# Clearing a dead strip on Pool between the row scatters of chunks 1 to 3 of an attention and mixture-of-experts kernel

## The chip, the cores and the metric

The kernel runs on one core of one Trainium2 chip. The metric is the device time in microseconds (us) of one execution; lower is better. Every run is also recorded with its span and with the clock that TensorE was granted, as a share of full speed. A run counts as slow when it is over 1.5% above the fastest of the same kernel. The numbered runs (e1 to e18) were made on four different chips of the same kind, here called 0, 3, 9 and 10; for the two profiles and the comparison of record the chip isn't noted. Kernels of one call share a chip and the runs of the kernel before on it.

## The reference

Attention over keys and values that a softened sorting matrix has mixed, then a one-expert-per-row feed-forward layer. Cut to what matters:

```python
# q, k, v: (4, 8, 768, 64); sort_net: (4, 8, 8, 8)
k_sorted = einsum('bhij,bhjcd->bhicd', P, k_b)      # P: five rounds of softmax on sort_net
v_sorted = einsum('bhij,bhjcd->bhicd', P, v_b)
attn = softmax(q_b @ k_sorted.T / 8)                # inside blocks of 96 rows
x = (attn @ v_sorted) as 3072 rows of 512
# feed-forward: 8 experts, 512 -> 1024 -> 512
e_idx = argmax(x @ w_gate + modality_bias[modality_id])
for e in range(8):
    rows = e_idx == e
    out[rows] = gate[rows] * (relu(x[rows] @ w1[e]) @ w2[e])
```

## The kernel before

The 3072 rows are handled as four chunks, m = 0 to 3. When a chunk's attention is done, `place(m)` computes for each row its place in a list sorted by expert, and Pool writes the rows there with eight indirect DMAs (row scatters) into a scratch tensor in HBM:

```python
def one(t):
    if t:
        nc.gpsimd.nop()
    ins = nc.gpsimd.indirect_dma_start(
        out=xs_dram, out_offset=bass.IndirectOffsetOnAxis(ap=dest[:, t:t + 1], axis=0),
        in_=xt.bitcast(I32)[:, t], in_offset=None)
    ...  # (cut) the scatters of all chunks write disjoint rows and don't wait for each other
for t in range(8):
    one(t)
```

`table(m)` then fixes which pieces ("slots" of 256 rows of one expert) are complete. Slots 0 and 1 need chunk 0, slots 2 and 3 chunk 1, slots 4 to 7 chunk 2, the rest chunk 3. SyncE fetches a slot's rows transposed, after all scatters of the chunk:

```python
def x_fetch(s, row, own, after=(), n=PR):
    i1 = nc.sync.dma_start_transpose(out=xT_b[s % NX][:, :, 0:n], in_=view.bitcast(BF16)[:, 0:Dm])
    ...  # (cut) i2: row ids and gates; both wait for the DMAs in `after` (the chunk's scatters)
```

TensorE runs a slot's first layer on these rows, woven between the attention of later chunks, then the second layer; Pool scatters the results (output scatters):

```python
def mL1(s, j):                 # first layer: the first reader of xT
    hp = mipsum.tile([128, 2, PR], FP32, tag="mi", name=f"hp{s}_{j}")
    for f in range(2):
        for c in range(4):
            nc.tensor.matmul(hp[:, f], w_at(...), xT_b[s % NX][:, c], ...)
def y_out(s, t, n, parts):     # output scatter, also on Pool's queue
    ...
    ins = nc.gpsimd.indirect_dma_start(out=out, ...)
```

In the views, scatters of rows write `xs_scratch`, output scatters write `out_dram`, the transposed fetch reads `xs_scratch` into `xT`, and the first layer is `hp<-xT,w`.

The softmax here doesn't subtract the row's maximum and nothing guards it: scores larger than these inputs give would overflow.

## Time and profile before

| | value |
|---|---|
| time, median of 3 runs | 200.24 us (198.29 to 200.55) |
| profiled run | 236.47 us, span 234.8, clock 0.828 |
| TensorE busy in the profile | 174.2 us |
| row scatters | 32, 922 ns each, 8 in a burst |

The profiled run is 36 us longer than the timed ones. Its page shows in two lines where it stood. The first is the granted TensorE clock in 40 equal slices of the span, in tenths. The second, a group line, gives the busy time, the mean of one in ns, then the idle time ahead of it and what ended most of it.

```profile
PEclk9979799555569999659999555999958999999955
...
L424 ACT ACTIVATE attnT<-sc 96x768 bf16<-96x768 f32 x32 | 25.9, 809 | 34.3 <-remote 21.9
```

ScalarE's exponentials wait 21.9 us for something that the trace can't name ("remote", though the kernel has one core), and the half-rate stretches ("5") lie where that happens. I call these stops freezes below.

### The profile page before, as it was taken

The page shows a single profiled execution, that of the slowest core. Times are in us where ns is not written, and L with a number is a line of the kernel's source. Part 1 is how long each engine was busy: PE and PEld are TensorE (multiplying, and loading weights), DVE is VectorE, ACT ScalarE, POOL GpSimd, SP SyncE. Part 2 cuts the span into 40 slices and gives each one's busy share as a digit, 9 for nine tenths or more (in the row PEclk, how much of TensorE's full clock was granted, in tenths as well). Part 3 has the DMA queues.
Part 4 walks back from the last instruction along what each step waited for, and adds up shares of the span by engine and source line. Part 5 has one row for each costly group of instructions (what it writes and reads, how often), then busy time and mean ns, then how long its engine had stood idle before and what let it go on. Part 6 is the DMA issues. An engine that isn't in the chain of part 4 may idle for free.

```text
span 234.8 us, 5146 instructions
## 1 busy us (share of the span) xinstructions
PE 174.2 (74%) x2045; PEld 125.0 (53%) x2045; DVE 102.0 (43%) x333; ACT 93.0 (40%) x148; POOL 83.6 (36%) x118
## 2 busy tenths in 40 slices
PE   6583987796289899049898059999749999999500
PEld 2243976685278776037575047667516676664100
DVE  5876678563077773225472213347112233232200
ACT  2144777283178684045553053344132332332100
POOL 7801879206600307700307710206731332233300
PEclk9979799555569999659999555999958999999955
DMA  5999999999707696350202273313537522212200
GB/s 75 212 223 193 215 223 214 200 218 207 196 0 94 102 191 138 112 134 3 89 3 63 72 164 65 92 45 130 155 81 177 134 73 91 89 52 87 91 9 0
DMA packets 30160, 27.66 MB, mean 118 GB/s; under 512 B 18831, under 2 KB 25775, under 8 KB 29872
## 3 DMA queue, kind: packets, MB, share of 16 engines
q0 software_dynamic: 11792, 23.10, 44.1%
q1 hardware_dynamic: 18336, 4.16, 9.7%
q8 instruction: 18, 0.29, 0.5%
q14 instruction: 14, 0.11, 0.2%
HBM read 27.35 MB, written 10.52 MB: 161 GB/s over the span
## 4 chain that ended last, share of the span: by engine, by line
PE 60%; DVE 12%; another core or an unknown queue 10%; issue 6%; ACT 6%; POOL 1%; POOLq 0%; ACTq 0%; DVEq 0%
PE yp L706 18%; PE hp L683 17%; PE va L375 4%; PE sc L418 4%; PE op L437 4%; PE gt L450 3%; PE lg L456 3%; PE ka L366 3%; DVE xb L441 2%; ACT attnT L424 2%; ACT v_sb L353 2%; DVE kT L353 1%; DVE hT L675 1%; DVE P_t L272 1%
## 5 line engine op out<-in xcount | busy, mean ns | idle before, releaser
L683 PE MATMUL hp<-xT,w 128*128 128x256 bf16 x384 | 51.4, 287 | 0.5 <-ACT hT L677 0.5
L697 POOL DMA_INDIRECT out_dram<-kvb,idg x25 | 24.6, 982 | 73.2 <-ACT kvb L693 47.5
L683 PEld LDWEIGHTS <-w 128*128 128x128 bf16 x384 | 37.7, 102 | 10.4 <-issue 1.7
L527 POOL DMA_INDIRECT xs_scratch<-xb,dest x32 | 29.5, 922 | 37.0 <-issue 36.4
L424 ACT ACTIVATE attnT<-sc 96x768 bf16<-96x768 f32 x32 | 25.9, 809 | 34.3 <-remote 21.9
L706 PE MATMUL yp<-w,qT 128*128 128x512 bf16 x96 | 24.8, 405 | 4.0 <-ACT hT L677 4.0
L418 PE MATMUL sc<-qT,kT 64*128 64x96 bf16 (+1 forms) x256 | 12.9, 226 | 17.5 <-ACT attnT L424 16.6
L706 PE MATMUL yp<-w,hT 128*128 128x512 bf16 x96 | 22.5, 379 | 0.0
L441 DVE TENSOR_TENSOR xb<-op,rs 96x512 bf16<-96x512 f32 x32 | 22.0, 687 | 1.2
L418 PEld LDWEIGHTS <-kT 64*128 64x128 bf16 (+1 forms) x256 | 7.9, 103 | 19.8 <-issue 18.0
L695 DVE TENSOR_SCALAR kvb<-yp,idg 128x512 f32<-128x512 f32 x11 | 8.3, 751 | 21.6 <-PE yp L706 21.6
L706 PEld LDWEIGHTS <-qT 128*128 128x128 bf16 x96 | 9.5, 103 | 14.4 <-issue 6.3
L677 ACT ACTIVATE qT<-hp 128x512 bf16<-128x512 f32 x16 | 9.5, 596 | 18.4 <-PE hp L683 17.3
L677 ACT ACTIVATE hT<-hp 128x512 bf16<-128x512 f32 x17 | 10.1, 595 | 16.6 <-PE hp L683 8.4
L437 PE MATMUL op<-v_sb,attnT 96*128 96x65 bf16 x256 | 15.3, 207 | 1.1 <-DVE xb L441 0.4
L440 DVE RECIPROCAL rs<-op 96x8 f32<-96x8 f32 x32 | 6.3, 198 | 22.5 <-PE sc L418 7.4
L693 ACT ACTIVATE kvb<-yp,idg 128x512 f32<-128x512 f32 x13 | 8.9, 687 | 17.0 <-PE yp L706 14.7
L456 PE MATMUL lg<-wgp,xTg 128*96 128x8 bf16 x128 | 9.2, 195 | 7.1 <-issue 6.0
L437 PEld LDWEIGHTS <-attnT 96*128 96x128 bf16 x256 | 12.6, 107 | 2.5 <-DVE xb L441 0.9
L706 PEld LDWEIGHTS <-hT 128*128 128x128 bf16 x96 | 9.0, 98 | 9.0
L375 PE MATMUL va<-bd,kvb 128*128 128x128 bf16 x128 | 13.8, 274 | 0.0
L456 PEld LDWEIGHTS <-xTg 128*96 128x96 bf16 x128 | 8.8, 141 | 9.3 <-issue 6.2
(179 smaller groups left out, 235.4 us busy)
## 6 DMA issues: line engine op xcount, KB each, us to landing
w<-in_moe_w_dram POOLq DMA_DIRECT2D x4, 1024.0 KB
kvb<-in_k_dram POOLq DMA_DIRECT2D x4, 768.0 KB
kvb<-in_v_dram POOLq DMA_DIRECT2D x2, 1536.0 KB
q_in<-in_q_dram POOLq DMA_DIRECT2D x4, 384.0 KB
xs_scratch<-zpad SPq DMA_DIRECT2D x3, 258.0 KB
v_sb<-in_q_dram POOLq DMA_DIRECT2D x4, 192.0 KB
v_sb<-in_q_dram POOLq DMA_DIRECT2D x2, 384.0 KB
xs_scratch<-xb,dest POOLq DMA_INDIRECT x32
```

The lines of the kernel that those rows point to most:

```text
L375: nc.tensor.matmul(acc[:, z], v_cols[:, d0 + z], bd[g], start=True, stop=True)
L418: nc.tensor.matmul(sc[0:m, par, j * BLK:(j + 1) * BLK], kT[g][rows, x0:x0 + m], qT[rows, i], start=True, stop=True)
L424: mark[0] = nc.scalar.activation(attnT[u % 2][:, 0:8 * BLK].rearrange("p (r f) -> p r f", r=2), sc_tiles.pop(u)[0:BLK, :, 0:4 * BLK], ACT. ...
L437: nc.tensor.matmul(ov[:, par, j], attnT[u % 2][:, c0:c0 + 128], v_sb[g][0:BLK, par * 64 + h * 8 + i, 0:D + 1], start=True, stop=True)
L441: nc.vector.tensor_tensor(xt[:, :, h * D:(h + 1) * D].rearrange("p (r j) d -> p r j d", r=2), ov[0:BLK, :, :, 0:D], rs.broadcast_to([BLK, ...
L456: nc.tensor.matmul(lg[:, t], xTg[c % 2][:, t], wgp[:, c], start=True, stop=True)
L527: ins = nc.gpsimd.indirect_dma_start(out=xs_dram, out_offset=bass.IndirectOffsetOnAxis(ap=dest[:, t:t + 1], axis=0), in_=xt.bitcast(I32)[: ...
L677: mark[0] = nc.scalar.activation(dst, src, ACT.Relu)
L683: nc.tensor.matmul(hp[:, f], w_at(s, c * F + (2 * j + f) * 128, 128), xT_b[s % NX][:, c], start=(c == 0), stop=(c == 3))
L693: nc.scalar.activation(dst, src, ACT.Copy, scale=gate)
L697: ins = nc.gpsimd.indirect_dma_start(out=out, out_offset=bass.IndirectOffsetOnAxis(ap=idg[:, t, 0:1], axis=0), in_=y, in_offset=None, boun ...
L706: nc.tensor.matmul(yp, hT_b[s % 2][:, fc, t * 128:(t + 1) * 128], w_at(s, 4 * F + fc * Dm, Dm), start=(fc == 0), stop=(fc == 7))
```

## The change

The intent is to spread the eight scatters of a burst: Pool clears a strip of a key buffer that nobody reads any more, so it has something to do for about half a microsecond between two scatters (0.55 us a clear in the profile after). Chunk 0 is left back to back.

```diff
         def one(t):
             if t:
+                if m:
+                    nc.gpsimd.memset(kT[0][:, 0:512], 0.0)
                 nc.gpsimd.nop()
             ins = nc.gpsimd.indirect_dma_start(
```

Nothing else changes; the order of instructions on the other four engines is the same.

## The prediction

> **What bounds the kernel now.** I read the busy shares first, then the chain of waits in order of time, then the timelines of Pool and SyncE, then Pool's groups by shape.

> ```profile
> PE 174.2 (74%) x2045; PEld 125.0 (53%) x2045; DVE 102.0 (43%) x333; ACT 93.0 (40%) x148; POOL 83.6 (36%) x118
> ```

> TensorE is the busiest engine; Pool is free for two thirds of the span. But the chain of waits (start, us, what) is broken three times by something without a name:

> ```profile
> 92.56 9.33 another core or an unknown queue
> ...
> 127.35 9.26 another core or an unknown queue
> ...
> 168.24 4.32 another core or an unknown queue
> ...
> 184.40 1.75 PE hp L683 x16
> ```

> The kernel has one core, so "another core" cannot be taken literally. Each of the three lies inside a burst of row scatters. Pool's timeline of the last burst (start, us, instruction, idle before it):

> ```profile
> 161.26 0.22 POOL L520 COPY xb<-idI 96x8 int32<-96x8 int32 x1
> 161.97 0.93 POOL L527 DMA_INDIRECT xs_scratch<-xb,dest  x1 [0.49 <-issue]
> 163.21 0.91 POOL L527 DMA_INDIRECT xs_scratch<-xb,dest  x1 [0.30 <-issue]
> ...
> 169.29 0.91 POOL L527 DMA_INDIRECT xs_scratch<-xb,dest  x1 [0.31 <-issue]
> 170.50 0.91 POOL L527 DMA_INDIRECT xs_scratch<-xb,dest  x1 [0.30 <-issue]
> ```

> Eight scatters leave at 1.22 us each. The bursts of chunks 1 and 2 run from 87.64 and 123.72 to last starts at 96.25 and 132.25. SyncE then loads a stage's rows back with a transposing DMA, which must wait for every scatter of the chunk:

> ```profile
> 173.34 1.27 SPq L650 DMA_TRANSPOSE xT<-xs_scratch  x1
> ```

> So here 2.84 us pass from the start of the last scatter to the transpose (the trace's landing records put the scatter's own arrival at 2.2 us), and the view of tile xT gives a transpose 3.2 us (median) from issue to landing.

> The timed run takes 200.24 us, the profiled one 236.47: **36 us exist only while the profiler runs.** In ACT's timeline it stands still from 127.35 to 136.69 though the scores it needs ended at 127.24, and the trace's semaphore records show TensorE's increments arriving late in the bursts (the one for scores of 91.82 at 101.9). From the bursts' first stall to the matmul clock's recovery I count, against the pace of the same code outside bursts: chunk 0 about 7 us, chunk 1 9.3, chunk 2 11.4, chunk 3 6.8; together 34.5. That is nearly all of the 36. I therefore choose to read these gaps as the recorder's own, and take them out of the timeline before judging the change.

> [...] the copies in this trace take 823 ns for 768 columns, near 0.9 with a start-up of 0.1 to 0.15 us taken off. [...]

> **The change part by part.** It removes nothing. It adds 21 clears (7 each in chunks 1, 2 and 3) of 128x512 bf16 on Pool; the order of instructions on the other four engines stays as it was. The strip is dead after the first half of the heads, so the first clear's wait for TensorE is long over, and each later clear waits only for the clear before it.

> One clear, from Pool's groups by shape:

> ```profile
> masks.py:65 POOL MEMSET maskUT<- 128x128 bf16 x1 | 0.3, 260 | 0.0
> L973 POOL MEMSET const-bfloat16-1.0<- 128x1 bf16 x1 | 0.1, 110 | 0.0
> ```

> 127 columns cost 150 ns, 1.18 ns each; 512 columns are then 0.110 + 511 x 1.18 ns = 0.71 us. At the copies' 0.9 ns it is 0.57. I take **0.6 us, an estimate**. A copy after a scatter starts with no gap (160.29 + 0.98 = 161.27, the copy at 161.26), so the 0.30 us belongs to the scatter and stays. The period becomes 1.22 + 0.6 = 1.8 us, the last scatter of a chunk starts 7 x 0.6 = **4.2 us later**, and Pool's busy time grows by 21 x 0.6 = 12.6 us, which costs nothing by itself.

> What counts is the slack between a stage's rows and TensorE's first matmul on them. Rows are there about 2.5 us (between 2.2 and 2.84) plus 3.2 after the last scatter starts, so 5.7:

> - Chunk 1 (slot 2): rows at 96.25 + 5.7 = 102.0. Its first matmul stands at 114.30; less the 9.3 of the stall, 105.0. Slack 3.0; late by 1.2. TensorE idles about 1 us for VectorE just after (1.02 before the matmul at 116.62), which can absorb half: **0.6 us**.
> - Chunk 2 (slot 4): rows at 132.25 + 5.7 = 138.0. First matmul 151.13, less 11.4 = 139.7. Slack 1.7; late by **2.5 us**. From 151 on TensorE has no idle time, and the gating of chunk 3 stands behind this matmul in its queue, so this is paid in full.
> - Chunk 3 (slot 8): rows at 170.50 + 5.7 = 176.2. First matmul 184.24, less 6.8 = 177.4. Slack 1.2; late by **3.0 us**, in full: the rest of the kernel is a solid run of matmuls. Slots 9 to 12 follow at about 3 us per transpose, while TensorE takes 6.96 us a slot, so only the first is late.

> Sum 6.1 us, so 206.3 if every term holds. The clock may drop for some us after such waits; I leave that out.

> **The rivals.** (a) *Hidden anyway.* If the timed run's slack is 2 us larger than I subtract, or a clear overlaps the 0.30 us before the next scatter, the lateness falls to 2 us per chunk and the loss to 0 to 2: 200 to 202. For it: the slacks are differences of large numbers, good to some 1.5 us. Against it: the two last stages run with TensorE full. (b) *The pauses relieve a real stall.* If TensorE's increments are held up by the bursts in timed runs too, pauses could let them through: each stall begins 3.6 to 6 us into a burst, after three to five scatters. At full strength that would be worth tens of us, 180 or less. Against it: 34.5 us of stall cannot be in a timed run that is 36 us shorter. A remnant of 1 us per burst would give 197 to 199. (c) *Pool becomes the bound.* It has 83.6 + 12.6 of 200 us; only the two output scatters behind each burst slip by 4.2 us, and eight output buffers stand behind them. Nothing to add. [...]

> **Range and chances.** The sum says +6.1, rival (a) +0 to 2, rival (b) -1 to -3. I give the full sum about half the weight, (a) two fifths, (b) the rest, and land at +3.8: **204.0 us**, range **199.8 to 207.5**. 2% is 4.0 us, so my middle lies right at the limit: slower 0.48, same 0.48, faster 0.04.

> **What would show it.** In the changed profile: clears near 0.6 us and scatters 1.8 us apart in chunks 1 to 3, chunk 0 still at 1.22; the first transposes of stages 1 to 3 about 4 us later behind their bursts' starts; TensorE waiting for rows of slots 4 and 8, where it waits for none now. If the unnamed gaps are the recorder's, they may shrink, so that the profiled span falls while the timed runs do not. What would make me wrong: clears far from 0.6 us, a scatter that starts sooner after a clear, slack larger than 4 us at slots 4 and 8, or a timed gain, which would mean that the stalls are real.

The sum: 0.6, 2.5 and 3.0 us for slots 2, 4 and 8 make 6.1, on 200.24 that is 206.3. That the recorder makes the gaps is the author's reading of the 36 us between the timed and the profiled run; the profile didn't show it.

## The result, and the profile after

The changed kernel took **213.78 us** (median of 4, 212.81 to 214.37) against 200.40 (198.29 to 201.24) of the kernel before in the same rounds: ratio 1.0672, 95% interval 1.0589 to 1.0756. Slower, and outside the predicted range. Ratios here are the mean time of one kernel's fast runs over that of the other's of the same rounds, so not quite the ratio of the medians.

The profiled run took 212.81 us with clock 0.876, just as long as the timed ones. Its chain of waits has no unnamed piece at chunks 1 to 3. What TensorE waited for (us in total, times, longest), from the view of waits:

```profile
PE hp L685 <- DMA xT<-xs_scratch: 8.7, 3, 3.5
```

The first layer waits three times for rows. Pool's groups by shape give the clear, and Pool's timeline (start, us, instruction, idle before it) shows the spacing at the start of chunk 1's burst and what follows its eighth scatter:

```profile
L527 POOL MEMSET kT<- 128x512 bf16 x21 | 11.5, 546 | 0.0
```

```profile
80.25 0.98 POOL L529 DMA_INDIRECT xs_scratch<-xb,dest  x1 [4.97 <-issue]
81.23 0.55 POOL L527 MEMSET kT<- 128x512 bf16 x1
81.95 0.96 POOL L529 DMA_INDIRECT xs_scratch<-xb,dest  x1 [0.18 <-issue]
...
91.83 0.91 POOL L529 DMA_INDIRECT xs_scratch<-xb,dest  x1 [0.17 <-issue]
93.05 1.01 POOL L699 DMA_INDIRECT out_dram<-kvb,idg  x1 [0.31 <-issue]
94.36 0.99 POOL L699 DMA_INDIRECT out_dram<-kvb,idg  x1 [0.30 <-ACT kvb L695]
```

A clear costs 0.55 us, but the idle time before the next scatter falls from 0.30 to 0.17. Then come four output scatters (93.05, 94.36, 95.65, 96.93), and among them SyncE's fetch of slot 2. SyncE's timeline shows the first fetches of the three stages, TensorE's timeline the first matmuls on them:

```profile
94.40 1.29 SPq L652 DMA_TRANSPOSE xT<-xs_scratch  x1
...
125.63 1.27 SPq L652 DMA_TRANSPOSE xT<-xs_scratch  x1
...
156.74 1.27 SPq L652 DMA_TRANSPOSE xT<-xs_scratch  x1
```

```profile
98.83 1.05 PE L685 MATMUL hp<-xT,w 128*128 128x256 bf16 x8 [2.58 <-DMA xT<-xs_scratch]
...
129.98 1.05 PE L685 MATMUL hp<-xT,w 128*128 128x256 bf16 x8 [3.48 <-DMA xT<-xs_scratch]
...
160.51 1.92 PE L685 MATMUL hp<-xT,w 128*128 128x256 bf16 x16 [2.63 <-DMA xT<-xs_scratch]
```

From fetch to matmul it takes 4.43, 4.35 and 3.77 us. After the first two waits the clock falls. The page's clock line:

```profile
PEclk9859679955699999999559999799999999999955
```

Between 92 us and the last stage the granted clock is half for 13.7 us in all, from 100.7 to 110.9 and from 131.4 to 134.8. From 199.7 us to the end it is half once more, but so it is in the kernel before (from 189.5 in e15 below); this tail is left out in what follows.

### The profile page after: what moved, and what is told of

The parts are those of the page before. It is cut to its first block, busy times and chain, and to the rows that moved or that the text cites. A ratio compares the mean times of both kernels' runs of the same rounds, so it can differ in the third digit from the quotient of the medians.

```text
span 210.9 us, 5167 instructions
## 1 busy us (share of the span) xinstructions
PE 169.5 (80%) x2045; PEld 122.5 (58%) x2045; DVE 103.7 (49%) x333; ACT 93.2 (44%) x148; POOL 94.9 (45%) x139
## 4 chain that ended last, share of the span: by engine, by line
PE 57%; DVE 10%; POOL 9%; issue 7%; DMA 7%; ACT 4%; POOLq 0%; DVEq 0%; SPq 0%; ACTq 0%
PE hp L685 18%; PE yp L708 16%; DMA xT<-xs_scratch 6%; PE va L375 4%; PE ka L366 3%; PE sc L418 3%; POOL xs_scratch L529 3%; PE gt L450 3%; PE lg L456 3%; DVE xb L441 3%; PE op L437 3%; POOL v_sb L120 2%; PE warm L249 2%; ACT v_sb L353 2%; POOL kT L527 2%
## 5 line engine op out<-in xcount | busy, mean ns | idle before, releaser
L424 ACT ACTIVATE attnT<-sc 96x768 bf16<-96x768 f32 x32 | 25.9, 809 | 13.4 <-PE sc L418 13.0
L708 PE MATMUL yp<-w,qT 128*128 128x512 bf16 x96 | 22.7, 379 | 0.0
L437 PE MATMUL op<-v_sb,attnT 96*128 96x65 bf16 x256 | 14.4, 202 | 0.8 <-DVE xb L441 0.4
L418 PE MATMUL sc<-qT,kT 64*128 64x96 bf16 (+1 forms) x256 | 12.7, 223 | 1.8 <-ACT attnT L424 0.9
L375 PE MATMUL va<-bd,kvb 128*128 128x128 bf16 x128 | 13.5, 269 | 0.0
L440 DVE RECIPROCAL rs<-op 96x8 f32<-96x8 f32 x32 | 6.4, 199 | 13.7 <-PE op L437 13.7
L437 PEld LDWEIGHTS <-attnT 96*128 96x128 bf16 x256 | 11.8, 103 | 1.9 <-DVE xb L441 0.8
L366 PE MATMUL ka<-bd,kvb 128*64 128x64 bf16 x384 | 9.6, 216 | 4.0 <-issue 2.8
L375 PEld LDWEIGHTS <-kvb 128*128 128x128 bf16 x128 | 12.6, 195 | 0.2
L450 PE MATMUL gt<-ident,xb 96*128 96x96 bf16 x128 | 9.4, 224 | 4.2 <-DVE xb L441 4.1
```

What stands on the lines that cost most here:

```text
L366: nc.tensor.matmul(acc[par * 64:(par + 1) * 64, z], k_raw[:, (c0 + z) * D:(c0 + z + 1) * D], bd[g][:, par * 64:(par + 1) * 64], start=True ...
L375: nc.tensor.matmul(acc[:, z], v_cols[:, d0 + z], bd[g], start=True, stop=True)
L418: nc.tensor.matmul(sc[0:m, par, j * BLK:(j + 1) * BLK], kT[g][rows, x0:x0 + m], qT[rows, i], start=True, stop=True)
L424: mark[0] = nc.scalar.activation(attnT[u % 2][:, 0:8 * BLK].rearrange("p (r f) -> p r f", r=2), sc_tiles.pop(u)[0:BLK, :, 0:4 * BLK], ACT. ...
L437: nc.tensor.matmul(ov[:, par, j], attnT[u % 2][:, c0:c0 + 128], v_sb[g][0:BLK, par * 64 + h * 8 + i, 0:D + 1], start=True, stop=True)
L450: nc.tensor.transpose(tp[:, t], xb[m % 2][:, t, c * 128:(c + 1) * 128], ident[:BLK, :BLK])
```

## The experiments

All kernels gave correct results. On chips 0 and 10 the kernel before takes 237 to 242 us and freezes; on chips 3 and 9 it takes 197 to 205 and doesn't. I number the kernels in the order in which they ran, and group them by question.

### Are the freezes made by the profiling, or real?

Two theories stood against each other: the recorder makes them, as I had predicted, or they are real stalls, which the pauses may relieve. The kernel before, unchanged (e1, with e7 and e14 the same):

> The unchanged kernel again, for a second profile and as the measure of noise: within 1% of before (about 200 us). If the unnamed gaps in the first profile of before (9.3, 9.3 and 4.3 us) are the recorder's and come and go, this profile has a span near 199 us and no such gaps; then its matmuls on slots 2, 4 and 8 should wait 0 to 1 us for rows. If the gaps belong to back-to-back scatters, they are here again, span near 235.

Measured on chip 0: 239.46 us against 239.18, ratio 1.003. The timed runs are as long as the profiled one. The chain of waits of that run:

```profile
59.40 6.48 another core or an unknown queue
96.76 7.92 another core or an unknown queue
130.46 10.57 another core or an unknown queue
170.92 5.06 another core or an unknown queue
```

So the freezes are in timed runs too, on that chip. The clears moved behind the eighth scatter (e2), and left in chunk 1 alone (e3):

```diff
-                if m:
-                    nc.gpsimd.memset(kT[0][:, 0:512], 0.0)      # e2, e6: none in the burst
+        if m:                                                    # after the loop over one(t)
+            for _ in range(7):
+                nc.gpsimd.memset(kT[0][:, 0:512], 0.0)
```

> The same 21 clears, but all 7 of a chunk behind its eighth scatter, so no scatter is later. Theory A (the clears cost because the last row scatter is 2.9 us later and TensorE then waits for rows and cools down): within 1% of before, about 200 us, no wait for rows above 1 us. Rival B (the clears cost by themselves[...]): about 213, as with the change. Rival C (Pool's queue as a whole is later, output scatters included): the output scatters are 3.8 us later here too, so also well above 200.

233.37 us, ratio 0.976: three freezes of 5.7, 7.8 and 5.1 us stay at chunks 1 to 3.

```diff
-                if m:
+                if m == 1:                                       # e3
```

> Clears in chunk 1 alone. Theory A: one wait for slot 2's rows of about 2.6 us and then a half-rate matmul clock for some 10 us, which costs about 4.4 us: +6 to +7 us, 206 to 207. If only the waits counted (no clock), +2.6. If lateness adds up only over all three chunks, about 200.

234.47 us, ratio 0.981. Only chunk 1's freeze is gone; the chain of waits still has "124.52 10.81" and "165.13 5.04" as unnamed pieces. The pause between two scatters ends the freeze of its own burst. What e3 was meant for, the cost of one wait for rows where nothing freezes, was not tried again. The changed kernel itself (e5 on chip 3, e11 on chip 10):

> The changed kernel again, because before took 237 to 241 us in all the runs beside the first four experiments, against 198 to 201 beside the measurement on record: a chip seems to have two states, one in which TensorE's increments freeze inside dense scatter bursts, one in which they do not. If the freezes are here (before near 239): theory D says that the pauses break the freezes of chunks 1 to 3, so the changed kernel is the faster one, 222 to 228, ratio 0.93 to 0.95, with a freeze left in chunk 0 alone. If they are not (before near 200): 213 to 214 as on record, with waits for rows of 2.6, 3.5 and 2.6 us.

215.52 us on chip 3, ratio 1.0745 (1.0605 to 1.0884), with waits for rows of 8.7 us and three stretches at half rate: the result repeated.

> The changed kernel again, to stand on the same chip as the three kernels run with it. Theory A: waits of the first matmuls of slots 2, 4 and 8 for the transposed rows sum to 7.5 to 9 us, two or three half-rate windows of 3.4 to 10 us follow them, transpose to first matmul is 3.7 to 4.5 us; 212 to 217 us where before is near 200, and 220 to 226 us where before is near 239. Rival: a sum of waits under 5 us.

222.01 us on chip 10, ratio **0.932** (0.922 to 0.942). There the change gains 6.8%, as it does away with three freezes and keeps only chunk 0's. Its named waits for rows were 5.9 us there, at slots 4 and 8, and not the 7.5 to 9 expected. At slot 2 the first matmul stands behind 1.23 us of idle time that the trace lays to nothing ("issue"), 4.56 us after the fetch began; no landing of that fetch is recorded, so it can't be told whether this too is a wait for rows. The sign of this change depends on the chip. The two remaining runs of the kernel before on freezing chips said the same as e1:

> The kernel before once more, unchanged, for a profile of it on a chip that does not freeze (the chip of the call that gave 198 to 205 us; this expectation counts only if the time before comes out near 200). Theory A (the rows of chunks 1 to 3 are already almost on the path before the change): the waits of the first matmuls of slots 2, 4 and 8 for the transposed rows sum to 0.5 to 2.5 us, no half-rate clock lies between 60 and 185 us, and the profiled span is 197 to 200 us. Rival (my prediction's slack of 3.0, 1.7 and 1.2 us): no wait for rows at any of the three slots. If the chip freezes, about 238 us and pauses of 5 to 10 us at chunks 1 to 3.

> The kernel before, unchanged. Theory A, on a chip that does not freeze: 197 to 202 us, waits for rows 0.5 to 2.5 us in all, no half-rate window between 60 and 185 us. Rival (my prediction's slack of 3.0, 1.7 and 1.2 us at slots 2, 4 and 8): no wait for rows at all. On a chip that freezes: 237 to 241 us, and TensorE stands for 5 to 10 us at each of chunks 1 to 3 with nothing named that it waits for.

They took 237.85 us on chip 0 and 240.35 on chip 10, frozen at chunks 1 to 3, ratios 0.997 and 1.006.

### What does the kernel before wait for where nothing freezes?

> The kernel before, unchanged, for a profile on a chip that does not freeze (it counts only if the time comes out near 200 us). Theory A: waits of the first matmuls of slots 2, 4 and 8 for the transposed rows of 0.5 to 2.5 us in all, no half-rate window between 60 and 185 us, transpose to first matmul 3.5 to 4.5 us, since the output scatters follow right behind the burst here too. Rival (my prediction's slack of 3.0, 1.7 and 1.2 us): no wait for rows at all. On a chip that freezes: 237 to 241 us with freezes at chunks 1 to 3.

Chip 9: 200.56 us, profiled 200.7, clock 0.890. This is the profile that I lacked when I predicted. Its page's clock line, its waits of TensorE, its timelines of Pool and SyncE around chunk 2's last scatter, and TensorE's first matmul on slot 4:

```profile
PEclk9859759975556999999999999999999999999955
```

```profile
PE hp L683 <- DMA xT<-xs_scratch: 1.5, 1, 1.5
```

```profile
114.91 0.91 POOL L527 DMA_INDIRECT xs_scratch<-xb,dest  x1 [0.30 <-issue]
116.12 1.00 POOL L697 DMA_INDIRECT out_dram<-kvb,idg  x1 [0.30 <-issue]
```

```profile
117.48 1.30 SPq L650 DMA_TRANSPOSE xT<-xs_scratch  x1
```

```profile
122.05 1.05 PE L683 MATMUL hp<-xT,w 128*128 128x256 bf16 x8 [1.47 <-DMA xT<-xs_scratch]
```

The rows of slot 4 come 7.14 us after the start of the last scatter (2.57 to the fetch, 4.57 from fetch to matmul), and TensorE already waits 1.47 us for them. It does not wait at slots 2 and 8, but nearly. The view of DMA transfers, asked for the first fetch of slot 2 (begun at 93.24) and of slot 8 (at 144.27) alone, gives the us from issue to landing; TensorE's timeline gives the matmuls:

```profile
xT<-xs_scratch SPq DMA_TRANSPOSE x1, 3.4
...
xT<-xs_scratch SPq DMA_TRANSPOSE x1, 4.0
```

```profile
96.99 1.05 PE L683 MATMUL hp<-xT,w 128*128 128x256 bf16 x8
...
148.32 1.92 PE L683 MATMUL hp<-xT,w 128*128 128x256 bf16 x16
```

So the rows of slot 2 landed 0.4 us before their matmul and those of slot 8 at the very moment. Between 72 us and the tail no stretch runs at half rate. My rival, slack at all three slots, fell: the slack is 0.4 us, none and none.

### Does the time follow the delay of the last scatter?

The clears behind the burst instead of inside it (e6) keep Pool just as busy:

> All 7 clears of a chunk behind its eighth scatter, again, hoping for a chip without freezes. There theory A (late rows) says within 1% of before, about 200; rival B (the clears cost by themselves) about 213. With freezes: 0.97 to 0.98 of before, as in the first try (the output scatters no longer close behind the burst).

Chip 3: 198.45 us, ratio 0.996 (0.988 to 1.004); waits for rows 1.0 us. Pool's added work by itself costs nothing that these runs can show. A strip of 128 columns (e10, e18):

```diff
-                    nc.gpsimd.memset(kT[0][:, 0:512], 0.0)
+                    nc.gpsimd.memset(kT[0][:, 0:128], 0.0)
```

> The changed kernel with a strip of 128 columns instead of 512, all else the same. Theory A (the delay of the last scatter makes the time): a clear of about 0.15 to 0.25 us, much of it inside the gap of 0.30 us that each scatter has anyway, so the last scatter is later by under 1 us a chunk, the waits for rows fall to 1 to 4 us, and the time is 199 to 205 us. Rival (that seven more Pool instructions between the scatters, not their length, cost the time): the time stays at 211 us or more.

> The changed kernel with a strip of 128 columns; the clear was measured at 0.22 us. On a chip that does not freeze, theory A (the delay makes the time): a scatter every 1.30 us instead of 1.21, the last one 0.6 us later a chunk, waits for rows 1 to 4 us in all, time 199 to 204 us, ratio 0.995 to 1.02. Rival (the number of Pool instructions counts, not their length): ratio 1.05 or more. On a chip that freezes: 233 to 236 us, as once before.

On chip 0: 234.6 us, ratio 0.980, chunk 1's and 2's freezes there at 6.5 and 8.6 us (chunk 3's is not on its chain), so a pause of this length hardly breaks them; as 200 us was expected of a chip that doesn't freeze, the run said nothing else. On chip 3: 202.68 us, ratio 1.021 (1.014 to 1.029), hardly above the 1.02 expected. Its groups by shape and its waits:

```profile
L527 POOL MEMSET kT<- 128x128 bf16 x21 | 4.8, 229 | 0.0
```

```profile
PE hp L685 <- DMA xT<-xs_scratch: 3.1, 3, 1.8
```

In chunk 2 the last scatter starts 9.16 us after the first, where the kernel before has 8.50 and the changed kernel 11.39. In chunk 3 it is much the same (9.15, 8.50 and 11.40); in chunk 1 the eighth scatter of e18 waits 0.68 us for a weight load besides. The small delay brings 1.6 us more of waits over the three chunks, the large one 7.2. The same 21 instructions cost less than a third when they are shorter (2.1% against 6.7 and 7.5%); their count is not the cause.

### How much is the half-rate clock?

Spare matmuls on a constant go ahead of the first matmul of slots 2, 4 and 8 (e4, e8, e13, e17), so that TensorE isn't idle while it waits; their result is overwritten:

```diff
         hp = mipsum.tile([128, 2, PR], FP32, tag="mi", name=f"hp{s}_{j}")
+        for _ in range({(2, 0): 10, (4, 0): 14, (8, 0): 10}.get((s, j), 0) if ... else 0):
+            nc.tensor.matmul(hp.rearrange("p a b -> p (a b)"), ones_bf, wsrc, start=True, stop=True)
```

> The changed kernel with 10, 14 and 10 spare 128x512 matmuls (0.216 us each) in front of the first matmul of slots 2, 4 and 8, written into the tile that the real ones then overwrite. They fill the waits of 2.6, 3.5 and 2.6 us and depend on no rows. Theory A with the clock as a cost of its own: the rows come no sooner, but the clock stays at full rate, so about 5 to 6 us less than the changed kernel: 207 to 209. If the waits alone make the loss and the cold clock is hidden: 213 to 214, or a little more.

> The changed kernel with 10, 14 and 10 spare 128x512 matmuls ahead of the first matmul of slots 2, 4 and 8, so that TensorE is not idle while it waits for the rows. Theory A (of the 13.5 us between the changed kernel and the clears-last one, 7.7 are waits for rows and 5.8 half-rate clock that follows the idle waits): the half-rate windows vanish between 90 and 140 us and the time is 207 to 210 us where the changed kernel gives 213 to 216, ratio to before 1.035 to 1.05. Rival (half rate comes from something else[...]): the half-rate windows stay and the time is 213 us or more, ratio 1.07 or more.

> The changed kernel with 10, 14 and 10 spare matmuls ahead of the first matmul of slots 2, 4 and 8. Theory A (about 5.8 us of the 13.5 us lost are half-rate clock behind the idle waits): no half-rate window behind the waits, 3 to 7 us faster than the changed kernel of the same call. Rival (half rate costs nothing net, since the rows bound the kernel anyway): within 2 us of the changed kernel.

These three fell on freezing chips: 223.29, 219.42 and 223.25 us (ratios 0.938 and 0.920, none for the third; of four runs each, three of the first and two of the third count as slow). Beside e13 ran the changed kernel itself, 222.01 us, so the gain of 3 to 7 us expected there did not come. Its profile gives a likely reason: behind its waits it had 6.8 us at half rate, not 13.7, so there was less to gain. These runs settle nothing. The fourth fell on chip 3:

> The changed kernel with 10, 14 and 10 spare matmuls ahead of the first matmul of slots 2, 4 and 8. On a chip that does not freeze (before near 200 us), theory A (about 5 us of the loss are half-rate clock behind the idle waits): no half-rate window between 90 and 185 us, 207 to 210 us, ratio to before 1.035 to 1.055 where the changed kernel has 1.067 and 1.075. Rival (half rate costs nothing net): ratio 1.065 or more. On a chip that freezes: 219 to 224 us, as twice before.

208.37 us, ratio **1.0503** (1.0437 to 1.0569), where the changed kernel has 1.0672 and 1.0745; theory A had put it at 1.035 to 1.055. TensorE's timeline at slot 2, and the page's clock line:

```profile
96.34 2.33 PE L686 MATMUL hp<-ones_bf 128*128 128x512 bf16 x10
99.12 1.03 PE L689 MATMUL hp<-xT,w 128*128 128x256 bf16 x8 [0.45 <-DMA xT<-xs_scratch]
```

```profile
PEclk9969889955559999999999999999999999999855
```

At all three slots the spare matmuls end before the rows land, so they delay nothing; the half rate behind the waits is gone. The rows come no sooner, yet the kernel gains 1.7 to 2.4% of some 200 us, **3.4 to 4.8 us** (by the two intervals give or take 2.1 and 3.1, as the runs compared are of different calls). That is what the half rate costs in the changed kernel, net; the rest of the loss, about 10 us, stays with the clock full.

```profile
97.29:100.70 3.41, 1.30 (x16) 1.08 (x16) 0.51 (x2) 0.60 (x1) 0.83 (x2) 1.00 1.10 307
158.72:162.14 3.42, 1.63 (x15) 1.47 (x16) 0.47 (x1) 0.00 (x0) 0.98 (x1) 1.00 1.06 281
```

The first was followed by half rate, the second not. So it is in the seven profiles on chips that don't freeze, between 75 and 180 us, with some 200 windows: half rate followed each of the eight in which TensorE was busy 1.04 to 1.44 us, and none of the others, busy 1.63 us or more. In a frozen profile the border lies higher: in that of the kernel before, half rate followed a window with 1.73 us busy (126.75 to 130.16). A wait of 1.46 us (slot 2 of e16) was enough together with one of 1.02 us soon after it; of the 2.63 us at slot 8 of the run of record, part lay in the window before, and that was not enough. How long the half rate lasts differs too: three windows (10.2 us) behind slot 2 of the run of record, though TensorE was fully busy from 102 us on, and one (3.4 us) behind slot 4. No run here shows what decides that.

### Do the output scatters slow the fetch?

In the changed kernel the burst ends so late that three or four results are ready, and their output scatters leave in one row beside the fetch. This is less new than it looks: at slots 4 and 8 the kernel before has output scatters beside the fetch too, and in e15 the fetches take 3.4, 4.57 and 4.0 us, against 4.43, 4.35 and 3.77 in the run of record. Only slot 2's became slower. From the start of the last scatter to the rows it takes 6.8, 7.1 and 6.9 us before, and 7.0, 6.9 and 6.6 after. Seven more clears behind the eighth scatter push them 4 us away (e9, e12, e16: the changed kernel plus the loop of e2):

> The changed kernel with seven more clears behind the eighth scatter of chunks 1 to 3, which push the output scatters that queue behind the burst some 4 us away from the fetch of the transposed rows. Theory A (in the changed kernel four output scatters right behind the burst collide with the transposes, which is why transpose to first matmul takes 4.4 us instead of 3.3): transpose to first matmul falls to about 3.3 us at slots 2, 4 and 8, the waits for rows fall from 8.7 us to 5 to 6.5, and the time is 209 to 212 us. Rival (the last scatter is simply later by 1 to 3 us and the transposes are no slower for the output scatters): transpose to first matmul stays at 4 us or more, the waits stay near 8.7 us and the time 213 us or more.

> The changed kernel with seven more clears behind the eighth scatter of chunks 1 to 3, so that the output scatters come after the fetch of the rows. Theory A (output scatters right behind the burst slow the transposes by about 1 us each): transpose to first matmul 3.2 to 3.4 us where the changed kernel has 3.7 to 4.5; waits for rows 2 to 4 us shorter; 2 to 5 us faster than the changed kernel of the same call. Rival (the 1 us saved is lost again because the output rows leave 4 us later): within 1 us of the changed kernel.

> The changed kernel with seven more clears behind the eighth scatter. On a chip that does not freeze, theory A (output scatters behind the burst slow the transposes by about 1 us each): waits for rows 4 to 6 us where the changed kernel has 8.7, time 208 to 212 us, ratio to before 1.04 to 1.06. Rival: waits near 8.7, 213 us or more, ratio 1.07. On a chip that freezes: 217 to 223 us, ratio 0.91 to 0.93, as twice before.

The first two fell on freezing chips: 220.81 us on chip 0 (ratio 0.921) and 218.60 on chip 10 (0.911), the latter beside the changed kernel's 222.01 (0.932). For slot 4 of those two, the fetch and the matmul, first the changed kernel on chip 10 (e11), then with the output scatters pushed away (e12):

```profile
131.38 1.33 SPq L652 DMA_TRANSPOSE xT<-xs_scratch  x1
```

```profile
135.97 1.83 PE L685 MATMUL hp<-xT,w 128*128 128x256 bf16 x8 [3.30 <-DMA xT<-xs_scratch]
```

```profile
133.12 1.27 SPq L655 DMA_TRANSPOSE xT<-xs_scratch  x1
```

```profile
136.28 1.89 PE L688 MATMUL hp<-xT,w 128*128 128x256 bf16 x8 [1.96 <-DMA xT<-xs_scratch]
```

4.59 us become 3.16 at slot 4, and likewise 3.77 become 3.15 at slot 8; e9 has 3.26 and 3.37. The time is 3.4 us shorter, within the 2 to 5 that theory A expected. On chip 9 (e16) fetch to matmul is 3.32, 3.23 and 3.28 us, the waits at slots 2, 4 and 8 are 1.46, 2.37 and 2.03, so 5.9 us instead of 8.7, and the time is 209.46 us, ratio 1.042 (1.025 to 1.059), all as theory A expected. The profiled run of e16 counts as slow by the 1.5% rule (210.73 us, the fastest took 206.40); the fast pair on chip 10 carries the argument alone. The collision is real and makes some 3 us of the waits of the changed kernel. It is not what the change added, since most of it was there before.

### The account

Spans of the profiles on chips that don't freeze, from the first scatter of chunk 1 to the end, so that the differing clock of chunk 0 stays out. One profile stands for each kernel, and runs of the kernel before differ by some 3 us. Half rate is the time at half clock from 92 us to the tail; half of it is what it would cost if TensorE were busy all through it (in the run of record the first layer's matmuls start 213 ns apart at half rate and 109 ns apart at the full one).

| kernel | span from there | above before | added waits for rows | half of half rate | sum |
|---|---|---|---|---|---|
| before (e15) | 117.9 | | (has 1.5) | 0 | |
| clears last (e6) | 116.6 | -1.3 | -0.4 | 0 | -0.4 |
| narrow strip (e18) | 119.4 | 1.5 | 1.6 | 0 | 1.6 |
| spare matmuls (e17) | 126.5 | 8.6 | 8.8, of it 7.8 filled | 0 | 8.8 |
| clears twice (e16, slow run) | 129.4 | 11.4 | 4.4 | 6.8 | 11.2 |
| changed (of record) | 130.7 | 12.7 | 7.2 | 6.8 | 14.0 |
| changed (e5) | 134.1 | 16.1 | 7.2 | 10.2 | 17.4 |

The two causes account for each kernel to within 1.3 us. The two runs of the changed kernel have the same waits and differ by 6.8 us of half rate and by 3.4 us of span. The sum of half the half rate (6.8 to 10.2) is above the net 3.4 to 4.8, since a slower TensorE also arrives later at its next wait: with a full clock the waits are 10.3 us, with the half rate 8.7.

No kernel here beats both. With clears twice the freezing chips have their lowest ratios (0.921 and 0.911; on chip 0 the spare matmuls do as well, 0.920), the others lose 4%; clears last are even with the kernel before (0.996) where nothing freezes and 2.4% faster where it does.

## Why the prediction was wrong

The mechanism of the full sum was right: the last scatters come later, and TensorE waits for the rows of slots 2, 4 and 8. What failed is the size of two of its terms. The slack, set at 3.0, 1.7 and 1.2 us, is 0.4 us, none and none; and the clock behind the waits, left out, costs 3.4 to 4.8 us.

- **"36 us exist only while the profiler runs"** failed. The profile and the times most likely came from chips of two kinds: on chips 0 and 10 timed runs freeze as well (239 us), on chips 3 and 9 profiled runs don't freeze (200.7 us). To leave the freezes out was right for the comparison of record, where nothing froze; the reason wasn't, and rival (b), "the pauses relieve a real stall", holds on the other chips, at 6.8%.
- **The slack of "3.0", "1.7" and "1.2" us** was the worst mis-sized term. Each was a difference of large numbers out of a frozen profile. On a chip that doesn't freeze (e15) the rows of slot 2 land 0.4 us early, those of slot 8 just in time, and TensorE waits 1.47 us at slot 4 before the change. Of 2.8 + 2.9 + 2.9 us of delay 7.2 came through as added waits.
- **"Rows are there about 2.5 us … plus 3.2 after the last scatter starts, so 5.7"**: 7.14 us at slot 4 before the change, 7.00, 6.91 and 6.63 after it. The 3.2 is a fetch with no output scatters beside it (3.15 to 3.3 us in e12 and e16); at slots 4 and 8 they lay beside it before the change as well, and it took 4.57 and 4.0 us in e15.
- **"0.6 us, an estimate", and "the 0.30 us belongs to the scatter and stays"**: 0.55 us, and 0.17 of the 0.30 stays. From 229 ns at 128 columns (e18) and 546 ns at 512 a column costs 0.83 ns, not the 1.18 read from two small clears. Scatters are 1.63 us apart, not 1.8, and a chunk's last one is 2.9 us later, not 4.2. This error went the other way and nearly cancelled the first ones: the sum of 6.1 us of waits stands against 7.2 measured, which is luck.
- **"The clock may drop for some us after such waits; I leave that out"**: this is the missing term of the sum, 3.4 to 4.8 us by e17. Even the full sum, 206.3, was therefore too low.
- **The shading from +6.1 to +3.8** gave weight to rival (a), a hidden delay. No run shows slack of that kind. The weights as written give about +3.3, not +3.8; that changes nothing here. The added waits, 7.2 us, and half of the half rate, 6.8, make 14.0, against 12.7 us of span between the profiles and 13.4 of time; the half rate itself varies from run to run (13.7 and 20.4 us of it in two profiles).
- Rival (c), Pool as the bound, stayed as small as predicted: e6 has the same 21 clears and ratio 0.996. As its clears lie behind the burst, what a clear costs other engines inside a burst isn't tested by itself; the account above leaves at most 1.3 us open.

What the freeze is stays open. It came within bursts of eight scatters with 0.30 us between them, on two of the four chips; clears of 0.55 us between them end it, clears of 0.22 hardly do. Not every stop lies in such a burst: in e9 an unnamed piece of 3.13 us (at 105.86) stands beside the output scatters behind chunk 1's cleared burst. Whether the recorder has a part in it can't be told, since every run here, timed or profiled, was recorded with its clock.

## What to carry to other kernels

When a profiled run is much longer than the timed ones, get a second profile before subtracting anything: here slacks of 1 to 3 us (3.0, 1.7 and 1.2 read, 0.4 and twice none found) didn't survive the subtraction of a 10 us stall. A delay on a transfer that TensorE awaits is to be priced at the delay less the slack of an undisturbed profile (here 7.2 us of added waits), and at the clock that drops behind the wait, if a profile shows that it does (here 3.4 to 4.8 us). And before blaming the change for what a slow transfer runs beside, look whether it ran beside it already: here it mostly did, and moving the output scatters away is a gain of its own.
